# A fused attention and maxout kernel: softmax sums inverted on chip by VectorE block transposes, and the second stage begun two quads sooner

## The chip, the cores and the metric

The kernel runs on one core of one Trainium2 chip. The metric is device time in microseconds (us) of one execution; a lower number is better. "Before" is the tuned kernel, "after" is the same kernel with the change. Each comparison runs both kernels alternately on one chip. Differences between two experiments are differences of medians that were often taken on different chips, where the kernel before lies between 372.45 and 373.60 us; below about 2 us they say nothing.

The engines are called by their profile names too: PE is TensorE, PEld its weight loads, DVE is VectorE, ACT is ScalarE, POOL is GpSimd, SP is SyncE.

## The reference, cut to what matters

```python
# q, k, v: [8, 12, 448, 64] f32;  w1, w2: [768, 1024];  w_out: [1024, 768];  cap = 30
s = (1 / sqrt(64)) * q @ k.transpose(0, 1, 3, 2)
s = cap * tanh(s / cap)
a = exp(s - s.max(-1, keepdims=True))
x = (a / (a.sum(-1, keepdims=True) + 1e-9)) @ v
x = x.transpose(0, 2, 1, 3).reshape(3584, 768)
return maximum(x @ w1, x @ w2) @ w_out          # f32 out
```

## The kernel before

Scores are bounded by the cap, so no maximum is subtracted. The maxout is rewritten: max(h1, h2) = relu(x (w1 - w2)) + x w2. So the kernel needs `wd = w1 - w2` (six subtracts of 128x1024 on VectorE) and `wm = w2 @ w_out` (a premultiply on TensorE), and the second stage is `relu(x wd) @ w_out + x wm`.

The attention runs in 24 *quads* `t` of two head pairs (`ab` = 0, 1). All second-stage matmuls, the w2 transposes and the premultiply are Python generators in a queue; `F(n)` deals `n` of them ("fills") between the attention's instructions, so that TensorE has work while ScalarE computes tanh and exp. VectorE takes its instructions in program order.

```python
def add(t, ab, step):                 # VectorE, from quad NS = 5 on: sums of the exponentials
    ...                               # step 0: e1 + e2, step 1: += e0, step 2: += the last (half) tile

def pv(t, ab):
    ps = pv_psum.tile([P, 512], f32, name="pv")
    ...                               # 6 + 1 matmuls: exponentials times v
    if ab:
        ss = pv_psum.tile([P, 512], f32, name="ss")
        ...                           # sums of four heads: ones [128 x 32] times esum
    nc.vector.tensor_copy(U[t][:, ab, :], ps[:, :S])                  # PV out of PSUM
    if ab:
        nc.vector.tensor_copy(st, ss[:, :S])
        nc.sync.dma_start(out=sums[t], in_=...)                       # 32 x 56

def invert(t):
    nc.vector.reciprocal(r, sums[t])
    nc.sync.dma_start(out=recd[t], in_=r)                             # to DRAM

def spread(t):                        # broadcast to 64 partitions each
    for h in range(2):
        nc.sync.dma_start(out=rec[t][...], in_=lines[h : h + 1, :, :].to_broadcast([64, 2, S]))

def normalize(t, ab, eng=nc.gpsimd):
    eng.tensor_mul(xT[b // 2][:, hp, cs], U[t][:, ab, :], rec[t][:, ab, :])

def moe(b):                           # the second stage of one batch entry, dealt by F
    for f in range(FC):               # 8 relu groups
        ps = mm_psum.tile([P, 512], f32, name="mm")                   # mm_psum has 2 buffers
        ...                           # 6 matmuls, a yield after each
        nc.vector.tensor_relu(g[:, f, cs], ps[:, :S])
    ...                               # then 3 or 4 row tiles x 2 halves of 6 + 8 matmuls,
                                      # each ended by a VectorE copy out of "mm"
```

The `mm` banks: transposes of q and k, w2 transposes, premultiply and second stage all share two of them, and every one is emptied by VectorE.

## Time and profile before

| | before |
|---|---|
| time, median of 4 runs | 372.45 us (371.75 to 372.76) |
| TensorE busy | 344.8 us, 92% |
| ScalarE busy | 281.5 us, 75% |
| VectorE busy | 231.5 us, 62% |
| GpSimd busy | 161.5 us, 43% |
| DMA | 71.6 MB |

I cut the run at the single-tile tanh of each quad (one per quad, easy to find in the timeline): the start up to the third of them (25.4 us from the first to the third), then 7 quads (86.6 us), then 14 quads (178.9 us), then a tail of second-stage work alone (68.7 us).

### The profile page before, as it was taken

The numbers are of one execution on the slowest core, as the hardware profiler recorded it, in microseconds if no ns is written. First come the engines' busy times: TensorE is split into PE (matmuls) and PEld (weight loads), VectorE is DVE, ScalarE is ACT, GpSimd is POOL, SyncE is SP. The second block draws the span as 40 slices with busy tenths as digits, with TensorE's granted clock in tenths as the row PEclk, the third lists the DMA queues.
The fourth block names the chain that finished last, engine by engine and source line by source line (L and its number), as shares of the span: only waits on it lengthen the run. The fifth ranks groups of instructions, "written<-read, shape, count | busy, mean of one in ns | idle before, by whom it ended". The sixth has DMA issues, their size and how long they took to land.

```text
span 372.9 us, 6501 instructions
## 1 busy us (share of the span) xinstructions
PE 344.8 (92%) x2454; PEld 165.2 (44%) x2454; DVE 231.5 (62%) x389; ACT 281.5 (75%) x265; POOL 161.5 (43%) x197
## 2 busy tenths in 40 slices
PE   4668897999999999999979999999999999999996
PEld 2223444444444444444434344534453445555553
DVE  4153557577886777767674687659767868533421
ACT  4996998899999989998978899988998993000000
POOL 4851168690864376234554554544644332220000
PEclk9999999999999999999998999999999999999999
DMA  7998899768799979999599968897998133512022
GB/s 260 327 241 186 324 274 274 149 145 189 190 238 238 212 188 252 202 209 251 145 230 239 261 189 193 220 235 214 216 261 200 53 92 129 150 45 86 0 86 84
DMA packets 101200, 71.56 MB, mean 192 GB/s; under 512 B 56496, under 2 KB 96176, under 8 KB 101168
## 3 DMA queue, kind: packets, MB, share of 16 engines
q1 hardware_dynamic: 99216, 67.99, 70.6%
q0 software_dynamic: 1952, 3.15, 4.6%
q8 instruction: 19, 0.31, 0.4%
q14 instruction: 13, 0.11, 0.1%
HBM read 53.48 MB, written 11.18 MB: 173 GB/s over the span
## 4 chain that ended last, share of the span: by engine, by line
PE 56%; ACT 15%; DMA 12%; DVE 8%; SPq 5%; issue 2%; POOL 2%; DVEq 0%; POOLq 0%; ACTq 0%
PE mm L416 14%; PE mm L401 12%; PE mm L413 10%; ACT expo L303 7%; ACT tanh L296 7%; PE pv L339 6%; PE s L295 5%; DMA qr<-in_q_dram 4%; DMA kr<-in_k_dram 3%; PE pv L353 3%; DMA qkT<-kqf 2%; PE ss L352 2%; PE mm L232 2%; DMA vr<-in_v_dram 1%; DMA rec_d<-rec_s 1%
## 5 line engine op out<-in xcount | busy, mean ns | idle before, releaser
L303 ACT ACTIVATE expo<-tanh 128x1792 bf16<-128x1792 bf16 (+1 forms) x96 | 144.8, 1509 | 0.1
L296 ACT ACTIVATE tanh<-s 128x896 bf16<-128x896 f32 x144 | 124.2, 915 | 26.1 <-PE s L295 24.6
L388 POOL TENSOR_TENSOR xT<-u,rec_b 128x448 bf16<-128x448 f32 x48 | 59.4, 1258 | 125.5 <-DMA rec_b<-rec_d 81.0
L416 PE MATMUL mm<-wo_sb,gT 128*128 128x384 bf16 x448 | 86.1, 328 | 0.0
L401 PE MATMUL mm<-xT,wd_sb 128*128 128x448 bf16 x384 | 79.3, 352 | 1.0 <-DVE osb L420 0.6
L356 DVE COPY u<-pv 128x448 f32<-128x448 f32 x48 | 30.0, 624 | 72.0 <-PE pv L353 70.5
L413 PE MATMUL mm<-wm_sb,xT 128*128 128x384 bf16 x336 | 67.9, 330 | 0.3 <-DVE gT L405 0.2
L416 PEld LDWEIGHTS <-gT 128*128 128x128 bf16 x448 | 43.6, 98 | 30.5 <-issue 2.9
L295 PE MATMUL s<-qkT 64*128 64x448 bf16 x288 | 43.8, 373 | 10.6 <-ACT tanh L298 3.9
L401 PEld LDWEIGHTS <-wd_sb 128*128 128x128 bf16 x384 | 37.0, 98 | 36.2 <-issue 4.5
L420 DVE COPY osb<-mm 128x384 f32<-128x384 f32 x56 | 30.9, 553 | 32.8 <-PE mm L416 32.3
L405 DVE TENSOR_SCALAR gT<-mm 128x448 bf16<-128x448 f32 x64 | 39.3, 617 | 11.5 <-PE mm L401 11.2
L413 PEld LDWEIGHTS <-xT 128*128 128x128 bf16 x336 | 32.9, 99 | 24.4 <-issue 3.4
L339 PE MATMUL pv<-expo,vp 128*64 128x448 bf16 x288 | 37.5, 370 | 0.7 <-DVE u L356 0.7
L322 DVE TENSOR_TENSOR esum<-esum,expo 64x896 bf16<-64x896 bf16 x38 | 29.1, 766 | 0.7
L326 DVE TENSOR_TENSOR esum<-esum,expo 128x896 bf16<-128x896 bf16 x38 | 28.3, 744 | 1.6
L324 DVE TENSOR_TENSOR esum<-expo 128x896 bf16<-128x896 bf16 x38 | 28.8, 757 | 0.0
L295 PEld LDWEIGHTS <-qkT 64*128 64x128 bf16 x288 | 9.6, 95 | 37.5 <-issue 29.5
L298 ACT ACTIVATE tanh<-s 128x896 bf16<-128x896 f32 x24 | 22.0, 916 | 2.5 <-PE s L290 1.9
L232 PE MATMUL mm<-wo_sb,w2T 128*128 128x384 bf16 x96 | 18.5, 326 | 4.7 <-DVE qkT L264 4.3
L339 PEld LDWEIGHTS <-vp 128*64 128x64 bf16 x288 | 12.6, 110 | 21.5 <-issue 16.7
L178 POOL CAST kqf<-kr 128x1152 bf16<-128x1152 f32 x12 | 16.1, 1342 | 5.3 <-DMA kr<-in_k_dram 4.4
(59 smaller groups left out, 246.9 us busy)
## 6 DMA issues: line engine op xcount, KB each, us to landing
rec_b<-rec_d SPq DMA_DIRECT2D x48, 224.0 KB
kr<-in_k_dram SPq DMA_DIRECT2D x12, 576.0 KB
qr<-in_q_dram SPq DMA_DIRECT2D x12, 576.0 KB
vr<-in_v_dram SPq DMA_DIRECT2D x12, 576.0 KB
out_dram<-osb SPq DMA_DIRECT2D x17, 384.0 KB
out_dram<-osb SPq DMA_DIRECT2D x22, 192.0 KB
osb<-in_moe_w_dram SPq DMA_DIRECT2D x6, 512.0 KB
vr<-in_v_dram SPq DMA_DIRECT2D x4, 672.0 KB
```

The source lines that it names most:

```text
L295: nc.tensor.matmul(s[:, h, :S], k0[r, j * P : (j + 1) * P], qTn[r, :])
L296: nc.scalar.activation(tanh[t, p][:, 2 * m : 2 * m + 2, :], s[:, :, :S], AF.Tanh, scale=scale / cap)
L303: nc.scalar.activation(expo[t, p], tanh[t, p][:, 0:n, :], AF.Exp, scale=float(cap))
L322: nc.vector.tensor_add(d, d, expo[t, 2][r, :, :])
L339: nc.tensor.matmul(ps[r, :S], vp[g % 2][:, 2 * n + h, j, :], e_of(t, ab, j)[:, h, :], start=(j == 0), stop=False)
L356: nc.vector.tensor_copy(U[t][:, ab, :], ps[:, :S])
L388: eng.tensor_mul(xT[b // 2][:, hp, cs], U[t][:, ab, :], rec[t][:, ab, :])
L401: nc.tensor.matmul(ps[:, :S], wd_sb[:, c, f * P : (f + 1) * P], x[:, c, cs], start=(c == 0), stop=(c == KC - 1))
L405: nc.vector.tensor_relu(g[:, f, cs], ps[:, :S])
L413: nc.tensor.matmul(ps[:, : DM // 2], x[:, c, ts], wm_sb[:, c, hs], start=(c == 0), stop=False)
L416: nc.tensor.matmul(ps[:, : DM // 2], g[:, f, ts], wo_sb[:, f, hs], start=False, stop=(f == FC - 1))
L420: nc.vector.tensor_copy(osb[:, hs], ps[:, : DM // 2])
```

## The change

The intent: drop the trip of the sums through DRAM (per quad two DMAs of 7 KB and two broadcasts of 224 KB, 11 MB of broadcasts in all), free GpSimd of the multiplies, and start the second stage two quads sooner so that its tail shrinks. Per head pair the sums are now made 64 columns wide; VectorE transposes them in 32x32 blocks out of PSUM, inverts one column per block, transposes these back *broadcast*, and multiplies PV straight out of PSUM. The first of the three adds goes to GpSimd. w2 and w_out are requested first thing on GpSimd's queue.

```diff
-    NS = 5
+    NS = 3
...
         if step == 0:
-            nc.vector.tensor_add(d, ...)
+            nc.gpsimd.tensor_add(d, e_of(t, ab, 1 if ab else 0), e_of(t, ab, 2 if ab else 1))
         elif step == 1:
             nc.vector.tensor_add(d, d, e_of(t, ab, 0 if ab else 2))
         else:
+            for h in range(2):                                   # was one add of 64 x 896
+                r = slice(64 * h, 64 * h + 64)
+                nc.vector.tensor_add(d[r, h, :], d[r, h, :], expo[t, 2][r, ab, :])
...
-        nc.vector.tensor_copy(U[t][:, ab, :], ps[:, :S])
-        ...                          # st copy, sums DMA; invert(), spread(), normalize()
+        nc.vector.transpose(st.rearrange("p b c -> p (b c)"), ss[:, :S])
+        yield
+        nc.vector.reciprocal(rs, st[:, :, 0:1])                  # 128 x 14
+        nc.vector.transpose(rb.rearrange("p (b c) -> p b c", c=32), rs.to_broadcast([P, NB, 32]))
+        yield
+        nc.vector.tensor_mul(xT[b // 2][:, hp, cs], ps[:, :S], rb)
...
+    for c in range(3):               # at the start, on SP's queue
+        load_w1(c)
...
+    for f in range(0, FC, 2):        # at the start, on GpSimd's queue, ahead of its constants
+        load_wo(f)
+    for c in range(KC):
+        load_w2(c)
     fill_const(nc.gpsimd, 1)
...
+        rate[0] = 1.4 if t < 4 else 1.25        # fills dealt per place
+        if t >= 3 and t % 3 == 0:
+            fill_q.append(moe(t // 3 - 1))
...
+        if t == 3:                   # the six subtracts, in two bursts of three
+            for c in range(3, KC):
+                subtract(c)
...
+        if t == 2:
+            for c in range(3):
+                subtract(c)
```

## The prediction

> **What bounds the kernel now.** I read the busy line first, then equal slices cut at quad ends, then the chain of waits, then single waits. The page's first line:
>
> ```profile
> PE 344.8 (92%) x2454; PEld 165.2 (44%) x2454; DVE 231.5 (62%) x389; ACT 281.5 (75%) x265; POOL 161.5 (43%) x197
> ```
>
> TensorE is the busiest, but a busy share mixes stages. A quad (four heads' scores, exponentials, sums and PV) can be followed by its one tanh of the single-tile scores (source line 298): these start at 13.3, 24.0, 38.7, 50.5, 63.9, 77.4, 89.9, 101.7, 113.5, 125.3 us and so on to 304.2. So I cut the run there; columns are stretch, length, then busy us (and instructions) of PE, PEld, DVE, ACT, POOL, then granted clock, DMA share, GB/s:
>
> ```profile
> 13.30:38.70 25.40, 18.52 (x216) 8.17 (x216) 10.40 (x17) 21.81 (x23) 11.82 (x19) 1.00 1.01 252
> 38.70:125.30 86.60, 80.19 (x676) 37.83 (x676) 59.33 (x94) 81.72 (x77) 49.23 (x57) 1.00 0.88 220
> 125.30:304.20 178.90, 175.07 (x1109) 80.35 (x1107) 126.48 (x209) 163.51 (x154) 85.42 (x97) 0.99 0.85 207
> 304.20:372.90 68.70, 65.21 (x394) 36.21 (x392) 30.53 (x53) 6.66 (x7) 8.02 (x7) 1.00 0.24 79
> ```
>
> In the first 38.7 us nothing but attention runs and ScalarE leads. From 38.7 on second-stage matmuls ("fills") are dealt into the attention. From 125 to 304 PE is 98% busy and ACT 91%: the two are nearly balanced, PE slightly ahead. After 304 there is only PE work: 362 fills are still undone. So a fill moved forward pays only if it lands where PE idles. Two such places show. In the chain of waits (start, us, what), and in the timeline:
>
> ```profile
> 57.90 3.99 DMA kr<-in_k_dram
> 61.89 0.55 DVE wm_sb L237
> 62.44 0.89 DVE wd_sb L214
> 63.32 0.84 issue
> 64.16 0.66 DVE qkT L264
> ...
> 64.86 1.78 PE mm L232 x10
> ```
>
> Here VectorE waits for a w1 chunk that stands late in the DMA queue, subtracts it (1.15 to 2.1 us each, six of them), and PE waits for the PSUM copy behind (the timeline puts this wait of L232 at 1.61 us). And at 194.7 PE waits for a transposing DMA:
>
> ```profile
> 194.71 0.55 PE L295 MATMUL s<-qkT 64*128 64x448 bf16 x4 [2.27 <-DMA qkT<-kqf]
> ```
>
> The quads ending at 203.5 and 217.0 took 15.9 and 13.5 us; the other twelve from 125 to 304 average 12.46, so this stall and the clock drop after it (0.83 in 190 to 200) cost some 3.7 us.
>
> **What the Trainium skill says.** (1) "TensorE: Matmul & The Clock Gate", Back-to-back issue gap: N/2.4 + 2.5 ns warm, 189 ns for 448 columns. The trace agrees: the chain at 319.40 has 48 matmuls of L401 in 9.08 us, 189 ns each; L416 with 384 columns takes 1.30 us for 8, 162.5 ns. (The group means of 352 and 328 ns include pipeline latency and are not used.) (2) "SBUF — State Buffer", two separate sides: a VectorE instruction with two SBUF inputs and a GpSimd one exclude each other for a whole instruction. The trace agrees: an add of 0.61 us (median) took 1.58 us while GpSimd held on:
>
> ```profile
> 105.90 2.61 POOL L388 TENSOR_TENSOR xT<-u,rec_b 128x448 bf16<-128x448 f32 x2 [3.72 <-DMA rec_b<-rec_d]
> 105.94 1.58 DVE L324 TENSOR_TENSOR esum<-expo 128x896 bf16<-128x896 bf16 x1
> ```
>
> (3) "VectorE: DVE Perf Modes", The three transpose paths: only 32x32 blocks, 311 ns for 128 columns of bf16. No transpose of VectorE is in this trace; I take one element per cycle plus the fixed cost of a PSUM copy of the same 448 columns, which took 625 ns here. (4) "GPSIMD Engine Reference", Elementwise: about 2.6 cycles per element at 1.2 GHz for two inputs, so 1.94 us for 896. The trace's 448-element multiply took 1.135 us; scaled without its fixed part of about 0.15 that gives 2.1 us.
>
> **The change part by part.** I counted instructions in both built programs.
>
> *VectorE.* Removed: PV copies 30.0, sum copies 14.7, reciprocals 11.6, and the first of the three adds 28.8 (to GpSimd): 85.1 us. Added per head pair: transpose from PSUM 0.62, reciprocal of 14 columns about 0.17 (a quarter of the 482 ns for 56, plus some fixed cost), broadcast transpose about 0.60, multiply out of PSUM 0.62: 2.0 us, times 48 is 97. The adds now start at quad 3 instead of 5 (42 instead of 38), and the 64x896 one is split in two of about 0.38 to 0.45: 57.4 before, 31 + 38 after. Sum: 231.5 - 85.1 + 97 + 12 = about 255 us. Per steady quad that is 4.0 (chain) + 2.8 (adds) + 2.9 (evacuations, 15 per 146 fills at 0.55 to 0.62) = 9.7 us before lock waits, about what it was (1.25 + 0.6 + 0.5 + 3.7 + 2.9 = 9.0).
>
> *GpSimd.* Loses the 48 multiplies (59.4), gains 42 adds of 2.1: about 190 us busy. It isn't the bound, but holds the shared pair longer.
>
> *DMA.* The 48 broadcasts of 224 KB (11 MB of 71.6), the sums and the reciprocals go, and with them the waits in the SP queue (27.0 us for rec_d, 25.6 for st, 14.8 for rec_s) that delayed the loads behind them. I expect the 194.7 us stall to go: -3.7.
>
> *TensorE sums.* 146 matmuls become 132, but 64 columns wide, so two side by side where four were: four took 0.31 us, a pair of 64-wide PV takes 0.23. Steady quads 0.46 instead of 0.31; quads 1 and 2 about 1.84 instead of 0.87.
>
> *Fills.* Units: 0.189 and 0.1625 as above, four scores 0.49, the full-height score pair 0.38, six PV 0.69, last PV 0.2, 27 transposes 0.70, a w2 transpose 0.055. Attention without sums: 3 x 0.49 + 0.38 + 2 x 0.69 + 2 x 0.2 = 3.63 us a quad.
> - 38.7 to 125.3 (7 quads). Before: 40 w2 transposes 2.2, 96 premultiplies 15.6, 64 + 84 second-stage 12.1 + 13.7, attention 25.4, sums 4.4, transposes 4.2: 77.6 us of 86.6, so 9.0 lost. After: 48, 96, and 96 + 106 second-stage: 2.6 + 15.6 + 18.1 + 17.2 + 25.4 + 5.3 + 4.2 = 88.4, and I add 3 for the subtracts, now two bursts of three (3.5 to 4 us each on VectorE): 91.4, +4.8.
> - 125.3 to 304.2 (14 quads). Before 658 fills of which 224 wide: 12.0 us of PE a quad, 12.46 taken. After 665 of which 192 wide: 12.17, so +0.17 x 14 = 2.4, less the stall 3.7: -1.3.
> - After 304.2: 301 fills instead of 362, all 61 narrow: 61 x 0.1625 = -9.9.
> - Before 38.7: weights now share the DMA engines with the first loads, and the first sums are slower at a cold clock: +1.
>
> Sum: 372.6 + 1 + 4.8 - 1.3 - 9.9 = 367.2, rounded to 367. The net gain is small because of the 61 fills moved from the end most land in quads that the old program had already filled to within 9 us.
>
> **The rivals.**
> 1. *VectorE becomes the bound.* A quad full of the relu evacuations (8 of 0.62) has 4.0 + 2.8 + 4.9 = 11.7 us of VectorE plus perhaps 2 of lock waits against 12.8 of PE. For: GpSimd busy about two thirds of a quad, four add groups exposed, single-buffered PV and sum banks now freed only by the multiply. Against: copies in a row start 0.54 apart, not 0.62. If so, +0.3 to 0.5 a quad in 14 quads and bursts of 3 more: 372 to 375.
> 2. *All idle time of PE goes.* If w1 at the start really ends the VectorE waits and the queue stalls, the early quads cost 89 and the steady ones 12.2: 361 to 363.
> 3. *The start starves.* w2 and w_out are requested at about 4.6 us on GpSimd, ahead of its constants and casts; DMA was already at share 1.01 from 13 to 39. A late q or k would idle ScalarE: +2 to 4, 369 to 371. Against: GpSimd's first cast of the second group had waited 2.2 us for its load and PE used it only at 17.5.
>
> **Range and chances.** Around 367, rival 2 pulls to 361, rivals 1 and 3 to 373. The 2% line is 365.1, between my sum and rival 2: faster by over 2% 0.33, within 2% 0.60, slower 0.07.
>
> **What would show it.** In the changed profile: no rec_b, sums or rec_d rows and about 60.5 MB; the PSUM transposes near 0.62 us and the broadcast ones near 0.60 (1.0 or more would make rival 1 true); GpSimd adds near 2.1; DVE near 255 us. The single-tile tanh of the last quad should start near 309 (304.2 + 1 + 4.8 - 1.3) and be followed by about 59 us; quads from 125 on should average 12.6. PE waits for VectorE (mm, pv) above 0.3 us a quad would show rival 1; tanh gaps before 38 us rival 3; no PE gap between 45 and 80 us rival 2. The prediction is wrong if a transpose costs something else than a copy, or if the hidden waits of PE in the old steady quads (0.46 each) came from the old VectorE order and vanish.

## More of the kernel before

From the waits of before, the line of how long ScalarE waited for scores (us in total, times, longest us):

```profile
ACT tanh L296 <- PE s L295: 24.6, 30, 4.7
```

One view is added here, because the result turns on it: two neighbouring steady quads of before, the first of which holds all eight relu groups of a second stage and the second none. Columns are the window, its length, busy us (and count) of PE, PEld, DVE, ACT, POOL, the granted clock, DMA share and GB/s:

```profile
203.53:217.01 13.48, 13.29 (x81) 5.71 (x80) 10.13 (x18) 11.68 (x11) 7.46 (x10) 1.00 0.89 229
217.01:229.01 12.00, 12.00 (x82) 5.79 (x81) 9.39 (x14) 11.68 (x11) 7.19 (x9) 1.00 0.78 202
```

In the plain quad TensorE never pauses. In the relu quad it pauses 0.19 us, with VectorE busy 10.13 us of 13.48, which is 75%. The 62% that the busy line gives for VectorE hide this.

## The result

| | before | after |
|---|---|---|
| median of 4 runs | 372.45 us | 395.46 us (394.44 to 396.48) |
| first to third single-tile tanh | 25.4 | 28.7 |
| next 7 quads | 86.6 | 107.6 |
| next 14 quads | 178.9 | 182.2 |
| tail | 68.7 | 60.6 |

The change costs 23 us. The ratio of after to before is 1.0609, with a 95% interval of 1.0574 to 1.0645. Ratios come from fast runs alone and are not quite the ratios of the medians quoted. The time lies outside the predicted range of 361 to 373. The stretches come from one profiled run of each kernel, with spans of 372.9 and 392.5 us, so their differences add to 19.6 us and not to the 23 of the medians.

The busy line of after, then the four stretches (columns as before):

```profile
PE 350.8 (89%) x2440; PEld 171.1 (44%) x2440; DVE 282.5 (72%) x497; ACT 281.5 (72%) x265; POOL 179.9 (46%) x191
```

```profile
13.40:42.05 28.65, 19.41 (x219) 9.27 (x219) 12.73 (x24) 21.75 (x22) 12.19 (x22) 1.00 1.08 303
42.05:149.62 107.57, 92.81 (x714) 45.17 (x712) 86.72 (x143) 81.76 (x78) 56.56 (x57) 0.97 0.55 149
149.62:331.86 182.24, 176.39 (x1115) 83.36 (x1113) 149.03 (x263) 163.51 (x154) 100.33 (x97) 1.00 0.58 158
331.86:392.50 60.64, 56.21 (x332) 30.55 (x330) 29.10 (x51) 6.65 (x6) 3.81 (x2) 1.00 0.15 53
```

Read the third column of numbers from the left in each (DVE) against the length: VectorE went from 59 of 86.6 us to 87 of 107.6 in the early quads, and from 126 to 149 in the steady ones. The tail is 8.1 us shorter, as wished; the early quads are 21 us longer. No engine is near 100% over the early stretch, and none was idle because work was lacking: this is a stretch of engines waiting for each other.

The groups of after that belong to the change (busy us, mean ns of one, then idle time just before them):

```profile
L318 POOL TENSOR_TENSOR esum<-expo 128x896 bf16<-128x896 bf16 x42 | 79.8, 1900 | 132.7 <-ACT expo L302 129.9
...
L325 DVE TENSOR_TENSOR esum<-esum,expo 64x448 bf16<-64x448 bf16 x84 | 54.0, 643 | 2.6
...
L356 DVE STREAM_TRANSPOSE st<-ss 128x448 f32<-128x448 f32 x48 | 31.1, 648 | 33.1 <-PE ss L346 24.4
...
L361 DVE STREAM_TRANSPOSE rb<-rs 128x448 f32<-128x448 f32 x48 | 31.0, 645 | 1.6
L366 DVE TENSOR_TENSOR xT<-pv,rb 128x448 bf16<-128x448 f32 x48 | 29.8, 620 | 3.1
```

The transposes cost what the prediction took. The halved add (L325) does not: 643 ns on average where 380 to 450 was expected. Its median is 390 ns, as expected, and its longest 2426. The timeline shows what makes the long ones, once GpSimd's add is running beside it:

```profile
228.78 1.88 POOL L318 TENSOR_TENSOR esum<-expo 128x896 bf16<-128x896 bf16 x1 [0.49 <-POOL vl L162]
229.16 2.17 DVE L325 TENSOR_TENSOR esum<-esum,expo 64x448 bf16<-64x448 bf16 x2
```

Two halves that take some 0.8 us together elsewhere stretch to 2.17 us, ending after GpSimd's 1.88 us.

Where the early quads lose their time, in the chain of waits (start, us, what) and the timeline of after:

```profile
57.11 4.87 DVE wd_sb L213 x3
61.97 0.56 DVE st L356
62.53 0.58 DVE w2T L223
63.11 0.16 DVE rs L359
...
70.29 0.65 DVE rb L361
...
71.93 4.50 DVE wd_sb L213 x3
76.43 1.00 DVE esum L320
77.43 0.48 DVE wm_sb L236
```

```profile
77.95 0.90 PE L261 MATMUL mm<-ident,kqf 64*64 64x64 bf16 x26 [5.36 <-DVE wm_sb L236]
...
82.11 1.73 ACT L295 ACTIVATE tanh<-s 128x896 bf16<-128x896 f32 x2 [6.92 <-PE s L294]
```

VectorE runs from 57 to 82 us with 2.4 us of pauses in all. Behind a burst of three subtracts stands the 0.48 us copy that empties an `mm` bank (`wm_sb` L236). TensorE needs that bank for the next transposes and stands for 5.36 us; then ScalarE, whose scores come behind them in TensorE's order, stands for 6.92 us. Over the whole run ScalarE's wait of this kind grew from 24.6 to:

```profile
ACT tanh L295 <- PE s L294: 43.8, 32, 6.9
```

The pause costs more than its length. The clock granted to TensorE (third number from the right) is down behind it, for four microseconds, and full again after:

```profile
77.95:82.00 4.05, 3.94 (x42) 2.21 (x41) 2.83 (x4) 0.00 (x0) 3.22 (x4) 0.52 0.90 232
82.00:93.77 11.77, 11.57 (x98) 5.55 (x95) 9.33 (x19) 9.18 (x10) 4.87 (x6) 1.00 0.01 1
```

What that is worth can be read from two later runs: e13's quad at this place (clock 0.84) keeps TensorE busy for 16.15 us, e15's with the same 141 matmuls (clock 1.00) for 14.38, so some 1.8 us.

The same mechanism, milder, in the two kinds of steady quad (the second holds seven of the eight relu groups):

```profile
241.33:253.41 12.08, 12.08 (x82) 5.92 (x80) 9.35 (x18) 11.68 (x11) 9.24 (x11) 1.00 0.43 86
253.41:267.98 14.57, 13.28 (x81) 5.79 (x80) 12.33 (x23) 11.68 (x11) 8.30 (x9) 1.00 1.02 263
```

The plain quad is still full of TensorE work. In the relu quad VectorE is busy 12.33 of 14.57 us and TensorE now loses 1.29 us. In the two that hold all eight groups VectorE is busy 13.38 of 14.94 and 12.14 of 14.02 us.

And the start: the timeline shows GpSimd held by its own DMA issues (L206 is a w2 load), so that its cast of the second group's k, and with it TensorE, came late:

```profile
17.23 0.53 POOL L206 DMA_DIRECT2D gT<-in_moe_w_dram  x1 [2.82 <-DMA wo_sb<-in_moe_w_out_dram]
...
19.68 1.14 POOL L170 CAST kqf<-kr 128x1152 bf16<-128x1152 f32 x1
...
20.87 0.53 PE L261 MATMUL mm<-ident,kqf 64*64 64x64 bf16 x12 [3.23 <-POOL kqf L170]
```

### The profile page after: what moved, and what is told of

Read it like the earlier page. It is cut to its first block, busy times and chain, and to the rows that moved or that the text cites. A ratio compares the mean times of both kernels' runs of the same rounds, so it can differ in the third digit from the quotient of the medians.

```text
span 392.5 us, 6409 instructions
## 1 busy us (share of the span) xinstructions
PE 350.8 (89%) x2440; PEld 171.1 (44%) x2440; DVE 282.5 (72%) x497; ACT 281.5 (72%) x265; POOL 179.9 (46%) x191
## 2 busy tenths in 40 slices
DMA packets 92271, 60.19 MB, mean 153 GB/s; under 512 B 53712, under 2 KB 87248, under 8 KB 92240
## 4 chain that ended last, share of the span: by engine, by line
PE 65%; DVE 20%; DMA 5%; ACT 4%; POOL 3%; issue 2%; SPq 1%; DVEq 0%; POOLq 0%; ACTq 0%
PE mm L394 15%; PE mm L379 13%; PE mm L391 12%; PE s L294 7%; PE pv L350 5%; DVE esum L325 4%; PE ss L346 3%; DVE esum L320 3%; DMA wo_sb<-in_moe_w_out_dram 3%; PE pv L353 3%; DVE wd_sb L213 2%; DVE gT L383 2%; PE mm L231 2%; DVE rb L361 2%; DMA qr<-in_q_dram 2%; ACT expo L302 2%
## 5 line engine op out<-in xcount | busy, mean ns | idle before, releaser
L318 POOL TENSOR_TENSOR esum<-expo 128x896 bf16<-128x896 bf16 x42 | 79.8, 1900 | 132.7 <-ACT expo L302 129.9
L391 PE MATMUL mm<-wm_sb,xT 128*128 128x384 bf16 x336 | 66.8, 326 | 0.0
L325 DVE TENSOR_TENSOR esum<-esum,expo 64x448 bf16<-64x448 bf16 x84 | 54.0, 643 | 2.6
L379 PEld LDWEIGHTS <-wd_sb 128*128 128x128 bf16 x384 | 37.0, 98 | 43.3 <-issue 12.1
L356 DVE STREAM_TRANSPOSE st<-ss 128x448 f32<-128x448 f32 x48 | 31.1, 648 | 33.1 <-PE ss L346 24.4
L350 PE MATMUL pv<-expo,vp 128*64 128x448 bf16 x288 | 37.8, 359 | 0.0
L320 DVE TENSOR_TENSOR esum<-esum,expo 128x896 bf16<-128x896 bf16 x42 | 32.1, 765 | 4.6 <-POOL esum L318 4.6
L361 DVE STREAM_TRANSPOSE rb<-rs 128x448 f32<-128x448 f32 x48 | 31.0, 645 | 1.6
L366 DVE TENSOR_TENSOR xT<-pv,rb 128x448 bf16<-128x448 f32 x48 | 29.8, 620 | 3.1
L261 PE MATMUL mm<-ident,kqf 64*64 64x64 bf16 x312 | 9.5, 217 | 15.5 <-DVE wm_sb L236 6.6
L350 PEld LDWEIGHTS <-vp 128*64 128x64 bf16 x288 | 17.2, 112 | 12.0 <-issue 3.3
## 6 DMA issues: line engine op xcount, KB each, us to landing
osb<-in_moe_w_dram SPq DMA_DIRECT2D x6, 512.0 KB, 13.3
```

What stands on the lines that cost most here:

```text
L318: nc.gpsimd.tensor_add(d, e_of(t, ab, 1 if ab else 0), e_of(t, ab, 2 if ab else 1))
L320: nc.vector.tensor_add(d, d, e_of(t, ab, 0 if ab else 2))
L325: nc.vector.tensor_add(d[r, h, :], d[r, h, :], expo[t, 2][r, ab, :])
L350: nc.tensor.matmul(ps[half_of[h], :S], vp[g % 2][:, 2 * n + h, j, :], e_of(t, ab, j)[:, h, :], start=(j == 0), stop=False)
L361: nc.vector.transpose(rb.rearrange("p (b c) -> p b c", c=32), rs.to_broadcast([P, NB, 32]))
L379: nc.tensor.matmul(ps[:, :S], wd_sb[:, c, f * P : (f + 1) * P], x[:, c, cs], start=(c == 0), stop=(c == KC - 1))
```

## The experiments

Theories at the outset, all for the same 23 us:

- **Queue**: VectorE has too much in its in-order queue. The inversion's chain is longer than the two copies that it replaced, and PSUM evacuations behind it are late. It shows as a cost of the inversion alone.
- **Bursts**: the cost is the two bursts of subtracts. Spreading them would bring most of the 21 us back.
- **Lock**: GpSimd's adds hold VectorE's adds.
- **Start**: GpSimd's early weight loads delay its casts.

All 18 runs, with their medians, ratios to before on the same chip, and stretches from one profile each. "Start" here is the start time of the third single-tile tanh (38.7 for before, 42.0 for after).

| run | us | ratio to before [95%] | start | early | steady | tail |
|---|---|---|---|---|---|---|
| before | 372.45 | 1 | 38.7 | 86.6 | 178.9 | 68.7 |
| after | 395.46 | 1.0609 [1.0574, 1.0645] | 42.0 | 107.6 | 182.2 | 60.6 |
| e1_spread_sub | 393.34 | 1.0571 [1.0515, 1.0627] | 40.2 | 108.5 | 182.2 | 60.6 |
| e2_loads_back | 391.60 | 1.0519 [1.0462, 1.0576] | 38.5 | 107.6 | 182.2 | 60.6 |
| e3_add_dve | 471.19 | 1.2620 [1.2529, 1.2710] | 41.7 | 128.1 | 240.7 | 62.7 |
| e4_spread_loads | 389.01 | 1.0461 [1.0393, 1.0529] | 38.7 | 108.5 | 182.2 | 60.7 |
| e5_invert_only | 383.77 | 1.0269 [1.0247, 1.0292] | 37.8 | 91.5 | 183.7 | 69.1 |
| e6_sums_on_pe | 391.41 | 1.0475 [1.0457, 1.0493] | 41.2 | 105.3 | 182.2 | 60.7 |
| e7_pool_sub | 388.87 | 1.0413 [1.0382, 1.0443] | 39.0 | 104.2 | 182.2 | 61.1 |
| e8_no_lock (wrong) | 381.15 | 1.0203 [1.0176, 1.0229] | 41.5 | 101.3 | 176.9 | 60.2 |
| e9_no_spread (wrong) | 386.00 | 1.0359 [1.0315, 1.0402] | 41.6 | 104.1 | 178.7 | 60.0 |
| e10_invert_no_lock (wrong) | 381.33 | 1.0233 [1.0190, 1.0276] | 38.8 | 90.5 | 181.9 | 68.7 |
| e11_invert_dve_late | 398.35 | 1.0682 [1.0611, 1.0753] | 38.1 | 93.2 | 192.3 | 69.6 |
| b1_w1_early | 373.43 | 1.0006 [0.9951, 1.0061] | 38.7 | 88.9 | 176.6 | 68.6 |
| e12_no_lock_no_spread (wrong) | 377.50 | 1.0128 [1.0075, 1.0181] | 41.7 | 100.6 | 174.0 | 59.7 |
| e13_last_add_on_pe | 388.90 | 1.0439 [1.0394, 1.0485] | 42.4 | 106.4 | 178.5 | 59.8 |
| e14_invert_two_off (wrong) | 373.83 | 1.0033 [0.9992, 1.0075] | 38.9 | 88.8 | 176.1 | 68.8 |
| b2_double_u | 389.47 | 1.0458 [1.0398, 1.0518] | 39.3 | 93.5 | 185.9 | 69.5 |
| b3_last_add_on_pe | 377.12 | 1.0107 [1.0079, 1.0136] | 38.6 | 88.2 | 180.1 | 69.0 |
| e15_mended | 376.32 | 1.0093 [1.0045, 1.0140] | 38.4 | 97.9 | 178.4 | 59.8 |

Names that begin with e1 to e4, e6 to e9, e12, e13 and e15 are edits of after; b1 to b3 are edits of before; e5 puts the inversion alone into before, and e10, e11 and e14 are edits of e5. "(wrong)" marks kernels that give a wrong result, to take a cost away without a race.

### e1_spread_sub: the subtracts dealt one by one

```diff
-        if t == 3:
-            for c in range(3, KC):
-                subtract(c)
+        if t in (2, 3):
+            subtract(2 * t - 3)
...
+        if t in (1, 2, 3):           # in place of the burst at t == 2
+            subtract(2 * t - 2)
...
+        if t == 3:
+            subtract(5)
```

> The changed kernel with its six wd subtracts dealt out one per half quad (quads 1 to 3) instead of two bursts of three. Burst theory: the bursts (4.9 and 4.6 us on VectorE, PE waits of 2.3 and 5.4 us, ScalarE waits of 3.7 and 6.9 us, then a cold clock) cost 8 to 12 us, so 384 to 387 us, and no quad between 55 and 110 us longer than 16 us. Rival (VectorE is simply overfull there, whatever the order of its work): the same work only lands elsewhere, 392 us or more. Lock theory (adds on GpSimd shut out VectorE): also 392 or more, since it touches nothing of that.

Measured: 393.34 us, ratio 1.0571, an interval that overlaps that of after; the early stretch is 108.5 against 107.6. The two longest early quads only moved (16.8 and 23.8 us where after has 17.6 and 21.1). As the whole loss the bursts theory falls: in this kernel it isn't the bunching. The six subtracts themselves are still on VectorE here; e7 and e15 take them off it.

### e2_loads_back: w2 and w_out requested where before requests them

```diff
-    for f in range(0, FC, 2):
-        load_wo(f)
-    for c in range(KC):
-        load_w2(c)
     fill_const(nc.gpsimd, 1)
+    load_w2(0)
+    load_w2(1)
...
     cast(nc.gpsimd, 1, "q")
+    for f in range(0, FC, 2):
+        load_wo(f)
+    for c in range(2, KC):
+        load_w2(c)
```

> The changed kernel with w2 and w_out asked for where the kernel before asks for them (two chunks of w2 after the GpSimd constants, the rest after the casts of the second group). Start theory: the ten issues hold GpSimd until 17.7 us and make its casts 8 to 10 us late; this costs the 3.6 us by which the second quad grew (14.3 instead of 10.7 us), so 391 to 392 us and a second quad near 11 us. Rival (the loads of w1 on the other queue starve q and k anyway): the second quad stays above 13 us and the time above 394.

Measured: 391.60 us. The third tanh starts at 38.5 instead of 42.0, nothing else changes. The early request of the weights costs 3.5 us, all of it at the start (3.9 by the medians, 3.4 by the ratios), and buys nothing later.

### e3_add_dve: the first add on VectorE, in the same place

```diff
-            nc.gpsimd.tensor_add(d, e_of(t, ab, 1 if ab else 0), e_of(t, ab, 2 if ab else 1))
+            nc.vector.tensor_add(d, e_of(t, ab, 1 if ab else 0), e_of(t, ab, 2 if ab else 1))
```

> The changed kernel with the first of the three adds back on VectorE (42 instructions, some 26 us more work for it, none for GpSimd). Lock theory: without the 1.9 us GpSimd adds the 64x448 adds fall from 643 ns towards 400 and the 128x896 ones towards 620, which returns about 20 + 6 us of VectorE time, and the time falls to 385 to 392. Rival (VectorE is bound by its own count of instructions): VectorE gets 26 us more, and the time rises to 398 to 408.

Measured: 471.19 us, and this test failed as a test. The place in the program that was chosen for GpSimd comes before the exponentials are ready, so on VectorE's in-order queue the add blocks everything behind it: the waits of this run have 90.0 us in 41 waits of VectorE for the exponentials. It says that an early wait on VectorE is ruinous here; whether the lock costs time it can't say.

### e4_spread_loads: e1 and e2 together

> Both the spread subtracts and the loads at their old place. If burst and start are separate losses their gains add: about 380 to 384 us. If the start only moves the same wait into the subtracts, it is no better than the spread subtracts alone (384 to 387). What is then left over 372 belongs to the VectorE load and the lock.

Its edit is those of e1 and e2. Measured: 389.01 us, above both of the ranges that were expected. The start is e2's (38.7) and the early stretch e1's (108.5): the loads give back their 3.5 us, spreading the subtracts gives nothing that the stretches show, and the early quads are still 22 us longer than before's.

### e5_invert_only: the inversion alone, in before

Sums 64 wide, transposes, reciprocal, multiply out of PSUM and the moved first add, as in after; loads, NS = 5, subtracts and the times of the second stages as in before. The rate of fills is set so that each quad gets as many as in before.

```diff
-    NS = 3
+    NS = 5
...
-        rate[0] = 1.4 if t < 4 else 1.25
-        if t >= 3 and t % 3 == 0:
+        rate[0] = 40 / 38 if t < 8 else 47 / 38
+        weights(i)
+        if t % 3 == 2 and t > 5:
             fill_q.append(moe(t // 3 - 1))
...                                  # subtracts and loads where before has them
```

> One part of the change alone: the sums inverted on chip, the first add on GpSimd and the multiply out of PSUM, but loads, subtracts, premultiplies, number of quads summed on TensorE (5) and start of the second stage at the places of the kernel before, with its number of fills per quad (40, then 47). Theory A (the early start is what hurts: it puts second-stage work into quads whose VectorE is full): 370 to 376 us, the seven early quads back near 88 us in all. Theory B (the inversion itself overfills VectorE, wherever the second stage starts): 384 us or more, with the early quads above 95.

Measured: 383.77 us, between the two theories (B's early quads above 95 did not come, they take 91.5). So the inversion alone costs 11.3 of the 23 us (10.0 by the ratio), and by difference the earlier second stage with its loads and subtracts the other 11.7; that part alone, in before, was not run. The inversion's part is in the early (+4.9) and the steady quads (+4.8; the profiled run is 9.2 us longer than before's). VectorE is busy 269.5 us against 231.5.

### e6_sums_on_pe: after with NS = 5

```diff
-    NS = 3
+    NS = 5
```

> The changed kernel with the sums of quads 3 and 4 made by TensorE again (as before the change) instead of by adds on GpSimd and VectorE. It takes 2 x 2.8 us of adds and their lock waits off VectorE and puts 2 x 1.4 us on TensorE, in the two longest quads (17.6 and 21.1 us). If VectorE sets the pace there: 384 to 390 us, those two quads 4 to 8 us shorter in all. If TensorE did: 397 or more.

Measured: 391.41 us, 4 us less than after, and short of what was expected: the two longest quads are only 0.6 us shorter in all (16.2 and 21.8). Quads 3 and 4 have no adds then, at the price of 24 more sum matmuls: TensorE 353.2 us instead of 350.8, VectorE 272.0 instead of 282.5. More TensorE work and less VectorE work is *faster* in the early quads (105.3 against 107.6).

### e7_pool_sub: the subtracts on GpSimd, with e2's loads

```diff
-        nc.vector.tensor_sub(wd_sb[:, c, :], w1_in[c], w2b[:, c, :])
+        nc.gpsimd.tensor_sub(wd_sb[:, c, :], w1_in[c], w2b[:, c, :])
...                                  # called at t == 1 and t == 2; loads as in e2
```

> The changed kernel with the loads at their old place (391.6 us) and, on top, the six subtracts on GpSimd in quads 1 and 2, where it idled and VectorE has no instruction with two SBUF inputs. 9.4 us of VectorE go from quads 2 and 3. If VectorE is overfull there (dealing the subtracts out gave 2 us only): 380 to 386 us. If the subtracts do not matter at all and the adds or the lock do: 389 or more.

Measured: 388.87 us; early 104.2, 3.4 us less than e2. Six subtracts of some 1.5 us each gone from VectorE's queue give back a third of their time, less than expected. Two early quads still take 20.5 and 14.8 us. The timeline of the first shows a flaw of the test: beside three subtracts on GpSimd and the add that follows them (56.0 to 64.7 us), an add on VectorE takes 2.30 us and a pair of halved ones 3.82, so a lock came in the place of the work. e15 has them before the adds begin.

### e8_no_lock: GpSimd writes a constant instead of adding (wrong)

```diff
-            nc.gpsimd.tensor_add(d, e_of(t, ab, 1 if ab else 0), e_of(t, ab, 2 if ab else 1))
+            nc.gpsimd.memset(d, 1.0)
```

> Wrong result on purpose: the changed kernel's GpSimd adds are replaced by a memset of the same tile, which reads nothing and waits for no exponential. Lock theory: the 64x448 adds fall from 643 to 400 to 480 ns and the 128x896 ones from 765 towards 650 (casts still hold the pair at times), some 18 us less VectorE, and the time falls to 380 to 387. If the lock waits lie where VectorE has slack: 392 or more.

Measured: 381.15 us, 14.3 less than after. The two groups concerned:

```profile
L318 POOL MEMSET esum<- 128x896 bf16 x42 | 34.2, 842 | 14.8 <-PE ss L346 14.1
L325 DVE TENSOR_TENSOR esum<-esum,expo 64x448 bf16<-64x448 bf16 x84 | 35.8, 426 | 2.6
```

The halved adds fall from 643 to 426 ns, into the predicted range. The Trainium skill says why a memset is a fair control, "SBUF — State Buffer", Who interferes with whom: a VectorE instruction with two SBUF inputs contends with a GpSimd instruction that reads SBUF, and not with one that only writes it; this run agrees, with the 426 ns above. The run takes away one more thing: the add waits for exponentials and the memset doesn't, so VectorE's 4.6 us of waits for GpSimd's result go too. How the 14.3 us split between lock and wait stays open.

### e9_no_spread: no broadcast transpose (wrong)

```diff
-        rb = rpool.tile([P, S], f32, name="rb")
-        nc.vector.transpose(rb.rearrange("p (b c) -> p b c", c=32), rs.to_broadcast([P, NB, 32]))
...
-        nc.vector.tensor_mul(xT[b // 2][:, hp, cs], ps[:, :S], rb)
+        nc.vector.tensor_mul(xT[b // 2][:, hp, cs], ps[:, :S], st.rearrange("p b c -> p (b c)"))
```

> Wrong result on purpose: the changed kernel without the broadcast transpose (48 instructions of 645 ns, 31 us of VectorE); the multiply takes the first transpose's output. If plain VectorE load sets the pace of the longest quads: 381 to 387 us, the relu quads (14.4 to 14.9 us) down to 13.5 or so. If only lock waits matter and VectorE has slack otherwise: 392 or more.

Measured: 386.00 us. Taking 31 us of VectorE work off (282.5 to 251.7) gives 9.5 us of time, of which 3.5 each in the early and the steady quads. It also frees the PV bank sooner, but that is not where TensorE stood: among the TensorE waits that the trace of after lists, none is for the multiply (L366) or the transpose (L356) that free the PV and sum banks.

### e10_invert_no_lock: e8's edit in e5 (wrong)

> Wrong result on purpose: the inversion alone (383.8 us) with its GpSimd adds made a memset that reads nothing. Lock theory for the first half of the loss (+11 us): 371 to 376 us. If the inversion loses by its longer chain on VectorE instead: 380 or more.

Measured: 381.33 us, 2.4 less than e5 (1.3 by the ratios, whose intervals overlap). With the second stage where before has it, GpSimd's adds cost little. The other 9 of the inversion's 11.3 us are then most likely the longer chain on VectorE; e14 tests that.

### e11_invert_dve_late: e5 with the first add on VectorE, late

```diff
-            nc.gpsimd.tensor_add(d, ...)
+            nc.vector.tensor_add(d, ...)
...
-        add(t, 1, 0)                  # before the exponentials are there
...
+        add(t, 1, 0)                  # directly ahead of step 1
         add(t, 1, 1)
```

> The inversion alone with the first adds back on VectorE, this time placed late, right before the second adds, so that they wait for no exponential (the run with them at the early place took 471 us, with 90 us of VectorE waits for ScalarE). If that earlier loss was the place and not the work: 378 to 388 us, VectorE waits for expo below 10 us, 64x448 adds near 400 ns. If VectorE cannot carry 26 us more: 395 or more.

Measured: 398.35 us, 14.6 more than e5, for 15 us more of VectorE work (284.3 against 269.5), and no lock by GpSimd's adds. This is e3's question without its flaw, asked in e5. It shows the queue theory at its barest: the steady quads take 192.3 us. An early relu quad of this run shows how it comes (timeline): TensorE stands 2.92 us for a relu that hasn't emptied its bank.

```profile
102.64 0.97 PE L391 MATMUL mm<-wm_sb,xT 128*128 128x384 bf16 x5 [2.92 <-DVE gT L383]
```

### b1_w1_early: before with the first three w1 chunks requested at the start

```diff
-        2: [(load, (3, "k")), (load, (3, "q")), (load_w1, (0,))],
-        3: [(load_w1, (1,)), (load_w1, (2,)), (load, (2, "v"))],
+        2: [(load, (3, "k")), (load, (3, "q"))],
+        3: [(load, (2, "v"))],
...
+    for c in range(3):
+        load_w1(c)
```

> The kernel before with one part of the change: the first three chunks of w1 asked for at the start. If the VectorE waits for w1 in quads 3 to 6 of the kernel before (PE waits of 1.6, 0.8, 0.8 and 1.4 us behind them) are real losses: 367 to 370 us. If the w1 loads at the start delay q and k instead, or the waits are covered: 372 or more.

Measured: 373.43 us, ratio 1.0006: nothing gained. The wait that the prediction showed at 57.9 us is still there. In the timeline of this run VectorE pauses for a PV result and TensorE's wait for the copy behind the subtract is the same 1.61 us:

```profile
61.89 0.62 DVE L356 COPY u<-pv 128x448 f32<-128x448 f32 x1 [2.23 <-PE pv L353]
...
65.40 1.79 PE L232 MATMUL mm<-wo_sb,w2T 128*128 128x384 bf16 x10 [1.61 <-DVE qkT L264]
```

The subtract in that place is the fourth, whose chunk b1 does not move, so this run alone does not clear w1. The trace of before does: VectorE is idle ahead of none of its six subtracts, and its pause of 2.23 us there, at 61.35, ends with a PV result too. The prediction had read a w1 load into a step of the chain that names a load of k.

### e12_no_lock_no_spread: e8 and e9 together (wrong)

> Wrong result on purpose: the changed kernel with both costs taken away, the GpSimd adds that read SBUF (alone -14.3 us) and the broadcast transpose (alone -9.5 us). If both are shares of one VectorE queue that was overfull, the gains overlap in part: 372 to 378 us. If they were independent waits on different paths they add to 371.5 or less. If a third cause held the early quads, it stays at 379 or more with the fifth and sixth quads still above 17 us.

Measured: 377.50 us, 18.0 less than after, where 14.3 and 9.5 would add to 23.8. Two independent costs would add; two loads on one overfull queue need not, because once the queue has room the rest is worth nothing. The steady quads (174.0) are then shorter than before's, and the early ones still 14 us longer. One of these takes 22.1 us: that of the second burst of subtracts, behind which TensorE stands for 5.51 us. So with the other two costs gone the burst is what is left there; a run with it spread was not made.

### e13_last_add_on_pe: the halved add replaced by two matmuls

```diff
-        if t < NS or t >= NQ:
+        if t < NS or t >= NQ or step == 2:
             return
...
+            for h in range(2):
+                nc.tensor.matmul(ss[half_of[h], :S], ones2[:, h, :], expo[t, 2][:, ab, :], start=False, stop=True)
```

> Correct result: the changed kernel with the third add of each head pair (84 VectorE instructions of 643 ns, 54 us with their lock waits) given to TensorE, which sums that tile with two more matmuls (one pair, 0.23 us, twice a quad: 10 us of PE in all). If VectorE sets the pace of the quads: 382 to 388 us, relu quads near 13.3 us, the others 0.3 longer. If TensorE does: 400 or more.

Measured: 388.90 us, a correct result, 6.6 less than after (0.9 more than the expected range), although TensorE has 3.6 us more to do. The early quads stay at 106.4 us; the gain is in the steady ones. In the relu quad TensorE does not pause any more (plain quad, then relu quad):

```profile
238.00:250.46 12.46, 12.46 (x86) 6.14 (x84) 6.87 (x14) 11.68 (x11) 9.22 (x12) 1.00 0.53 138
250.46:263.96 13.50, 13.50 (x85) 6.02 (x84) 10.04 (x19) 11.69 (x11) 7.94 (x8) 1.00 1.00 259
```

In the relu quad VectorE falls to 10.04 us of 13.50 and the quad takes 13.50 instead of 14.57. The plain quad pays 0.38 us for the matmuls, since TensorE was full there.

### e14_invert_two_off: e5 without lock and broadcast (wrong)

Its edits are those of e8 and e9, in e5.

> Wrong result on purpose: the inversion alone (383.8 us) with the GpSimd adds a memset (alone -2.4) and without the broadcast transpose. If the rest of its loss is the length of the VectorE chain: 371 to 376 us. If it is something else (the sums in two-way tiles on PE, or the places of adds and fills): 378 or more.

Measured: 373.83 us, ratio 1.0033: before's time. The busy line shows VectorE at 226.9 us, where before has 231.5:

```profile
PE 347.1 (93%) x2464; PEld 169.9 (46%) x2464; DVE 226.9 (61%) x437; ACT 281.7 (76%) x265; POOL 130.9 (35%) x187
```

So the inversion's other parts (wider sums, multiply out of PSUM, no U buffers, no DMA) are neutral in sum; what costs is the VectorE time that it adds.

### b2_double_u: before, with the copy of PV done twice

```diff
         nc.vector.tensor_copy(U[t][:, ab, :], ps[:, :S])
+        nc.vector.tensor_copy(U[t][:, ab, :], ps[:, :S])
```

> The kernel before with a cost doubled: every PV copy out of PSUM is made twice (48 more VectorE instructions of 0.62 us, 30 us, about the net VectorE work that the inversion added). If VectorE work as such costs time once its queue is this full: 378 to 383 us. If the kernel before has slack for it: 372 to 375, and the loss of the inversion must come from its waits or places.

Measured: 389.47 us with a correct result: 17 us more for some 30 us of added copies on an engine that was 62% busy.

```profile
PE 347.2 (89%) x2454; PEld 164.9 (42%) x2454; DVE 259.1 (67%) x437; ACT 281.6 (73%) x265; POOL 158.1 (41%) x197
```

It has none of the change in it, so it shows the sensitivity of the old kernel by itself, larger than the 378 to 383 us expected. The second copy also frees the PV bank 0.6 us later, but the waits say that this is the smaller part: TensorE's wait for that bank goes from 0.7 to 1.4 us, its wait for `mm` banks in the second stage from 0.8 to 11.8, of which

```profile
PE mm L402 <- DVE gT L406: 8.6, 14, 2.1
```

Its relu quads take 15.4 to 17.5 us.

### b3_last_add_on_pe: before, with its third add as matmuls

```diff
-        if t < NS or t >= NQ:
+        if t < NS or t >= NQ or step == 2:
             return
...
-            for m in range(2 if t < NS else 0):
+            for m in range(2):
```

> Correct result: the kernel before with its third add (38 VectorE instructions of 766 ns, 29 us) given to TensorE as two more matmuls a quad for the sums (0.23 us x 19 = 4.4 us of PE). Doubling the PV copies showed 30 us more VectorE work to cost 17 us. If the price holds in the other direction too: 356 to 366 us. If the kernel before sits just at the knee (VectorE waits only begin above its load) the added TensorE work shows alone: 374 to 378.

Measured: 377.12 us, ratio 1.0107. VectorE falls from 231.5 to 209.1 us and nothing is gained; the 4.7 us are about what the matmuls add to TensorE (344.8 to 348.5 us busy). With b2 this brackets before: less VectorE work gains nothing, more of it costs at once. Before sits at the knee.

### e15_mended: after with what the runs taught

e2's loads, e13's matmuls, the subtracts on GpSimd in quads 1 and 2 (before its adds begin), and six buffers for w1 instead of three.

```diff
-    opool = ctx.enter_context(tc.tile_pool(name="opool", bufs=3))
+    opool = ctx.enter_context(tc.tile_pool(name="opool", bufs=6))
...                                  # and the edits of e2, e7 (subtracts) and e13
```

> Correct result: the changed kernel with all that helped, and the subtracts taken off VectorE for good: loads at their old place, third add on TensorE, six buffers for w1 so that no load waits for a subtract, and the six subtracts on GpSimd in quads 1 and 2 ahead of its first add. If the bursts and the start are what holds the early quads (20 us over), and VectorE work the rest: 374 to 380 us, the seven early quads below 97 us in all. If the early quads stay long without them: 383 or more, and their cause stays open.

Measured: 376.32 us, ratio 1.0093 [1.0045, 1.0140], correct. 19 of the 23 us are back, but it does not beat before; the early quads miss the expected 97 by 0.9. Against e13 they are 8.5 us shorter, so the subtracts on VectorE were a part of the early loss (the six buffers came with them and are not separated). Its early and steady stretches:

```profile
38.40:136.30 97.90, 92.14 (x736) 45.41 (x734) 65.88 (x114) 81.76 (x77) 58.26 (x61) 1.00 0.63 175
136.30:314.76 178.46, 178.46 (x1171) 85.35 (x1170) 111.58 (x207) 163.52 (x155) 99.62 (x96) 1.00 0.59 161
```

In the 14 steady quads TensorE is busy without a gap: nothing is left to win there but TensorE work. The early quads take 97.9 us. The prediction's unit times give 88.4 us of TensorE work for them, and the added matmuls make 2.3 more (6 quads of two pairs at 0.19), so some 7 us are lost, about as in before (9.0). Against before, the tail is 8.9 us shorter and the early quads are 11.3 longer: with most of the waits gone, moving second-stage work forward is an exchange.

## Why the prediction was wrong

**The failed step is VectorE's room.** The prediction compared VectorE's mean load per steady quad, 9.7 us after and 9.0 before, called it "about what it was", and so charged the early quads only "I add 3 for the subtracts ... 91.4, +4.8", and the steady ones "-1.3". Measured are +21.0 and +3.3. A mean of 9 in a quad of 12.5 looks like 3 us of room. It isn't, because VectorE's queue is in order and the two `mm` banks leave TensorE little to do while an evacuation waits its turn. b2 and b3 show that before had no room: 30 us more VectorE work cost 17 us, and 22 us less gained nothing.

- **The early quads (+4.8 predicted, +21.0 measured).** The term for TensorE's work, 88.4 us, is not refuted; e15 comes within 7 us of it plus its added matmuls. The term for what is lost beside it was mis-sized: 3 on top of no other loss, against 107.6 - 88.4 = 19 us. The sum also dropped the 9.0 us that before already lost there, as though late w1 chunks had caused them; in before's trace no subtract waits for its chunk, and b1, with three of the chunks early, loses as much. Of the 19 us some 1.8 are the slow clock behind the longest pause. The bursts were 4.87 and 4.50 us instead of "3.5 to 4", but e1 shows that bunching was not the point: it was the whole queue, the chain and the adds together with the subtracts (e7, e8, e9, e12 and e15 each take a part off and each gain).
- **The steady quads (-1.3 predicted, +3.3 measured).** The stretch was priced by its average quad. Its ten plain quads average 12.4 us, as cheap as hoped. Its four relu quads average 14.6 us, where the prediction's 12.8 of TensorE work plus the usual half microsecond would be 13.3: 4 times 1.3 is 5.2 us, about the 4.6 that are missing. e13 takes them to 13.3 to 13.5. The 3.7 us credited for the stall are no sum of the figures beside them (those give 4.5), but the size is right: b1's profile has no such stall, and its quad there takes 12.1 us instead of 15.9. Since b1's time is before's all the same, it is not shown that the median of before held the stall.
- **VectorE's sum (255 predicted, 282.5 measured).** Transposes (0.648 and 0.645 against 0.62 and 0.60) and the multiply (0.620) were right. The reciprocal took 0.241 instead of 0.17, 3 us in all. The halved adds took 54.0 instead of 38 us, the plain cost (median 390 ns) being right: "before lock waits" was said and the lock left out of the sum. e8 puts them at 35.8 us without it.
- **Rival 1 was the right one.** "VectorE becomes the bound" gave the mechanism and even its load in a relu quad, 11.7 plus locks, against 12.1 to 13.4 measured. Its sign came true: TensorE's waits for `mm` banks of the transposes and the second stage (6.6, 5.2 and 2.4 us) make 0.6 us a quad, where 0.3 was to show it. Its price, 0.3 to 0.5 a quad and 3 for the bursts, was too small by a factor of about four. It should have been worked out like the main line, from the relu quads and the early ones rather than from an average.
- **Rival 3 was right in size**: 2 to 4 us at the start; e2 and the start of after say 3.4 to 3.9. (The cold clock that the main line assumes at the start is not there: 1.00 is granted from 4 us to the third tanh in both traces.) The prediction thought of late loads of q and k; the trace puts it down to GpSimd, held at its own DMA issues, so that its casts came late.
- **The tail and the DMA were right.** The tail is 60.6 (about 59 predicted), DMA moved 60.19 MB (60.5), and the stall of 194.7 us on a transposing DMA is gone. The last single-tile tanh, expected near 309, starts at 331.86.
- **The moved fills** ("most land in quads that the old program had already filled"): right, and stronger than said. e15 has the waits mended and still trades 8.9 us in the tail for 11.3 in the early quads.

By cause, as far as shown: the inversion alone 10.0 to 11.3 us (e5), nearly all of it VectorE time (e14 is back at before's time); the earlier start, by difference, the rest, of which 3.4 to 3.9 are the loads (e2). Within the whole change GpSimd's adds account for 14.3 us with the wait that they bring (e8) and the broadcast transpose for 9.5 (e9), together 18.0 (e12); these overlap with the first split and are not to be added to it. Open: how much of e8 is lock and how much wait, why the two costs add up to less than their sum in just that measure, how much of the early loss is the subtracts and how much the rest of the queue, and how e15's last 3.7 us divide between added sum matmuls and early quads.

## What to carry to other kernels

Do not read room from the mean busy share of an engine whose queue is in order and which empties other engines' buffers: cut the run into its kinds of stretch, and look at the fullest one, here the quad with seven or eight relu evacuations, where VectorE went from 9.8 to 10.1 us before to 12.1 to 13.4 after. A cheap test before such a change is to double one harmless instruction of that engine: b2 cost one line, and would have foretold that 30 us more on a "62% busy" engine cost 17. And work moved off a DMA that only an engine with time to spare waits for (GpSimd, 43% busy, 81.0 us of waits for the broadcasts) was no gain here, but a load on the engine that took it.

## What the Trainium skill lacked or had wrong

- "VectorE: DVE Perf Modes", The three transpose paths: it gives no time for f32 or for a wider tile. Here 32x32-block transposes of 128x448 f32 took 648 ns out of PSUM and 645 ns from a broadcast SBUF operand, as much as a copy or multiply of the same columns (620 ns).
- No page that I found gives VectorE's reciprocal by size. Here 14 columns on 128 partitions took 241 ns and 56 columns on 32 partitions 482 ns: about 5.7 ns a column over some 160 ns, if the two sizes lie on one line and the partitions don't count.
- "GPSIMD Engine Reference", Elementwise: 2.6 cycles per element at 1.2 GHz, a figure for f32, would make 1.94 us (an estimate) for 896 bf16 elements, before any fixed part. The add took 1.90 us with its fixed part, so the rate is lower here (about 2.3 if the fixed part is the 0.15 us that the prediction took).
- No page that I found says how many DMAs GpSimd can have requested before it must wait. Here the ninth and tenth of ten in a row waited 3.5 and 2.8 us for earlier ones, and held GpSimd's casts until 19.7 us. Whether the chip sets that number or the program's own semaphores do is not shown.
